# Causal mask by TensorE, one-row loads and a new order in a one-core attention and feed-forward kernel

## The chip, the cores and the metric

The kernel runs on one core of a Trainium2 chip. Each core has a matrix engine (TensorE, PE in the profile), a vector engine (VectorE, DVE), a scalar engine (ScalarE, ACT), a general one (GpSimd, POOL) and a queue engine (SyncE, SP), which work side by side and wait for each other by semaphores; 16 DMA engines move data between the main memory and the core's own memory. The metric is the device time of one execution in microseconds, the median of the runs; less is better.

## The reference

Eight batches of eight heads, 576 positions, head size 64, all float32. Causal attention with a decay that is worked out from f, then a gated feed-forward block on the 4608 tokens:

```python
log_f = np.log(np.clip(f, 0.0001, 1.0))
cum = np.cumsum(log_f, axis=-1)
scores = q @ k.T / sqrt(64) + (cum[:, :, :, None] - cum[:, :, None, :])
scores = np.where(causal, -1e9, scores)
attn = softmax(scores) @ v                       # 8 x 8 x 576 x 64
x = attn.transpose(0, 2, 1, 3).reshape(4608, 512)
xn = x / sqrt(mean(x * x) + 1e-6) * rms_g
out = (silu(xn @ w_gate) * (xn @ w_val)) @ w_out   # 512 -> 1536 -> 512
```

The decay of the key's position is multiplied into v (tile Vs, by decT) and into a column of ones beside it, so that the query's part cancels in the division; scores need no addition for it.

## The kernel before

**Tiles.** A block (b, qi) is 128 queries of all eight heads of batch b; a batch has four such blocks and a last one of 64 queries, which is joined with that of the next batch. For every block the kernel loads q, k and v, turns q and k (`turn_pe`: transposes on PE and copies by DVE and ACT, for the first eight blocks of the kernel, set by `onpe`; `turn`: a DMA transpose issued by SP, for the others), multiplies scores into a PSUM tile sc of two banks (`score_block`, L569), takes exp on ACT (L588) into PT, masks the diagonal tile, multiplies with Vs (`values`, L622, a unit for the even heads and one for the odd ones), divides (L637, L639), and norms: the sum of squares (L653 on ACT or L667 on DVE), its power on POOL (L672), xn (L679 or L683), and a transpose into xT (L692 and L699 for the first two groups, a DMA transpose at L703 otherwise).

**Groups.** Four blocks of 128 tokens make a group of 512 tokens; there are nine, the ninth from the blocks of 64. The first four blocks are block 0 of batches 0 to 3. For each group `gate` makes hidden columns from w_gate and w_val (L771; twelve gates, in the first two groups cut into tokens halves x = 0 and 1, where x = 0 needs only the first two blocks), with tanh on ACT (L784) and two products on DVE (L786, L778), and `project` multiplies by w_out (L802), copies on ACT (L814) and stores (L820, L828). The last project, of group 8, is done in two halves of 256 columns.

**The masks.** The four blocks of the first group (`FAST`) are masked on DVE by a minimum with the tile keep (L602), all later diagonal tiles on POOL (L596).

**The loads of the start.** POOL issues the q and k loads, which cast to bfloat16, and the weights; SP issues f, four v loads and rgT. For block 0 of batches 0 to 3 the q and k loads take two neighbouring rows of a head at once (`paired`, L391): 512 pieces of 512 bytes into the tiles `T_two`, which lie over ores, ga and th, turned by 16 transposes of 64 x 64 (L511). The other q and k loads take one row of a head at a time: 1024 pieces of 256 bytes (L398).

**The order.** All work is entered as units with an engine, an assumed duration, a key, dependencies and ring buffers (`Hold`). `Plan.run` plays them through once on the host: whenever an engine is free it takes the ready unit with the smallest key whose buffers are free. The order so found is the program's order on every engine. The key of each unit is moved by a number of the list SHIFTS (in hundredths of a group). The durations in the units only set this order; the chip takes its own.

Of the kernel before, what the change touches and what calls it, by code (L numbers as in the profile page):

```python
# [10 lines left out]
BF16 = mybir.dt.bfloat16  # L11
# [201 lines left out]
def fox_ffn_kernel(ctx, tc, q, k, v, f, moe_w_gate, moe_w_val, moe_w_out, moe_rms_g, out):  # L213
# [70 lines left out]

    issues = {}

    def load(eng, issue, moves, key, emit, deps=(), take=(), give=(), late=1.45):


        lane = Hold("sw" if eng == "POOL" else "hw", 1)  # L290
# [603 lines left out]
```

## Time and profile before

| | us |
|---|---|
| median of three runs | 375.93 (375.31 to 381.64) |
| the profiled execution | 376.78 |
| its span, first to last instruction | 375.1 |
| PE busy | 351.7 |
| exp on ACT (L588), 100 tiles | 99.4 |
| gate products on DVE (L786, L778) | 146.5 |
| first gate matmul (L771) | starts at 24.07 |
| last copy (L814) | starts at 371.09 |

The page's first part has the busy time of each engine; its second part cuts the span in 40 slices of about 9.4 us, each digit the busy share in tenths. A view of windows gives the same in us for chosen stretches, followed by the granted clock of PE, the DMA share and GB/s. The timeline lists instructions with their start, their duration and, in brackets, the idle time of the engine ahead of them and what ended it. The chain of waits follows the work that ended last back to the start. A tile's view gives the minimum, the median and the maximum of its instructions in ns, and the time from a DMA's issue to its landing. In the DMA view a queue q0 is that of POOL's loads and q1 that of SP's.

### The profile page before, as it was taken

The numbers are of one execution on the slowest core, as the hardware profiler recorded it, in microseconds if no ns is written. First come the engines' busy times: TensorE is split into PE (matmuls) and PEld (weight loads), VectorE is DVE, ScalarE is ACT, GpSimd is POOL, SyncE is SP. The second block draws the span as 40 slices with busy tenths as digits, with TensorE's granted clock in tenths as the row PEclk, the third lists the DMA queues.
The fourth block names the chain that finished last, engine by engine and source line by source line (L and its number), as shares of the span: only waits on it lengthen the run. The fifth ranks groups of instructions, "written<-read, shape, count | busy, mean of one in ns | idle before, by whom it ended". The sixth has DMA issues, their size and how long they took to land.

```text
span 375.1 us, 8971 instructions
## 1 busy us (share of the span) xinstructions
PE 351.7 (94%) x3569; PEld 203.7 (54%) x3617; DVE 237.1 (63%) x460; ACT 206.7 (55%) x310; POOL 190.3 (51%) x259
## 2 busy tenths in 40 slices
PE   2669999999999998999999999999999999999995
PEld 2548876677755555545455455445455544444453
DVE  6758776599766857666545667655467782473520
ACT  5544666686677657735675667336777331333122
POOL 8776999999899738843534396424112000000000
PEclk9999999999999999999999999999999999999998
DMA  9999999999999959993958999960602000201024
GB/s 127 178 204 212 207 190 166 196 152 128 161 173 183 156 84 178 179 187 63 192 97 93 165 124 139 182 100 31 136 8 56 2 16 29 82 3 56 18 49 102
DMA packets 152922, 45.05 MB, mean 120 GB/s; under 512 B 141424, under 2 KB 147312, under 8 KB 152880
## 3 DMA queue, kind: packets, MB, share of 16 engines
q0 software_dynamic: 77856, 17.83, 53.9%
q1 hardware_dynamic: 74944, 26.58, 37.0%
q8 instruction: 28, 0.46, 0.5%
q14 instruction: 14, 0.11, 0.1%
q10 hardware_dynamic: 80, 0.07, 0.1%
HBM read 38.16 MB, written 9.44 MB: 127 GB/s over the span
## 4 chain that ended last, share of the span: by engine, by line
PE 85%; DVE 6%; DMA 5%; issue 2%; ACT 1%; POOL 1%; ACTq 0%; DVEq 0%; SPq 0%
PE ff L771 47%; PE ff L802 24%; PE sc L569 7%; PE ff L622 6%; DMA rgT<-in_moe_rms_g_dram 3%; DMA QT<-qk 2%; DVE junk L667 1%; DVE x L639 1%; DVE ga L786 1%; DVE hT L778 1%; DVE Vs L327 1%; DVE xn L683 1%; PE ff L692 0%; POOL rs L672 0%; PE ff L515 0%
## 5 line engine op out<-in xcount | busy, mean ns | idle before, releaser
L588 ACT ACTIVATE PT<-sc 128x1024 bf16<-128x1024 f32 x100 | 99.4, 1022 | 41.2 <-PE sc L569 35.5
L786 DVE SCALAR_TENSOR_TENSOR ga<-th,ff 128x512 f32<-128x512 f32 x108 | 73.6, 685 | 55.2 <-ACT th L784 51.1
L802 PE MATMUL ff<-wo,hT 128*128 128x512 bf16 (+1 forms) x421 | 102.2, 373 | 1.5 <-issue 0.5
L784 ACT ACTIVATE th<-ff 128x512 f32<-128x512 f32 x108 | 64.2, 598 | 64.5 <-PE ff L771 55.5
L771 PE MATMUL ff<-xT,wg 128*128 128x512 bf16 (+1 forms) x465 | 94.0, 340 | 2.5 <-DVE rden L637 0.9
L771 PE MATMUL ff<-xT,wv 128*128 128x512 bf16 (+1 forms) x472 | 94.1, 337 | 0.8 <-DVE hT L778 0.2
L778 DVE SCALAR_TENSOR_TENSOR hT<-ga,ff 128x512 bf16<-128x512 f32 x108 | 72.9, 685 | 26.9 <-PE ff L771 20.5
L771 PEld LDWEIGHTS <-wg 128*128 128x128 bf16 x528 | 50.2, 99 | 41.7 <-issue 2.2
L771 PEld LDWEIGHTS <-wv 128*128 128x128 bf16 x528 | 50.4, 98 | 40.3 <-issue 0.3
L802 PEld LDWEIGHTS <-hT 128*128 128x128 bf16 x444 | 40.5, 98 | 41.2
L596 POOL TENSOR_SCALAR_AFFINE_SELECT PT<-PT 128x1024 bf16<-128x1024 bf16 x32 | 36.2, 1134 | 41.9 <-ACT PT L588 38.7
L540 POOL TENSOR_TENSOR Vs<-v,decT 128x512 bf16<-128x512 f32 (+1 forms) x39 | 41.7, 1069 | 24.7 <-DMA v<-in_v_dram 24.1
L814 ACT COPY ores<-ff 128x512 f32<-128x512 f32 (+1 forms) x37 | 21.1, 572 | 39.5 <-PE ff L802 39.4
L622 PEld LDWEIGHTS <-PT 128*128 128x128 bf16 (+1 forms) x960 | 32.8, 103 | 17.4 <-issue 7.2
L622 PE MATMUL ff<-Vs,PT 128*128 128x65 bf16 (+1 forms) x960 | 36.9, 196 | 4.3 <-POOL Vs L541 3.0
L672 POOL TENSOR_TENSOR rs<-ms,mhalf 128x1 f32<-128x1 f32 (+1 forms) x28 | 17.9, 639 | 38.4 <-ACT junk L653 34.5
L569 PE MATMUL sc<-QT,KT 64*128 64x128 bf16 (+1 forms) x960 | 32.4, 211 | 3.7 <-DVE rgT L321 1.8
L569 PEld LDWEIGHTS <-KT 64*128 64x128 bf16 x960 | 24.0, 95 | 18.1 <-issue 14.3
L639 DVE TENSOR_TENSOR x<-ff,rden 128x256 f32<-128x256 f32 x72 | 30.6, 424 | 2.5
L398 POOL DMA_DIRECT2D qk<-in_q_dram x36 | 31.3, 873 | 0.6 <-issue 0.5
L398 POOL DMA_DIRECT2D qk<-in_k_dram x36 | 31.3, 872 | 0.3 <-DMA wo<-in_moe_w_out_dram 0.3
L683 DVE SCALAR_TENSOR_TENSOR xn<-x,rs,rgB 128x512 bf16<-128x512 f32 x28 | 24.4, 898 | 10.6 <-POOL rs L672 10.6
(67 smaller groups left out, 165.0 us busy)
## 6 DMA issues: line engine op xcount, KB each, us to landing
out_dram<-ores SPq DMA_DIRECT2D x32, 256.0 KB, 2.4
v<-in_v_dram SPq DMA_DIRECT2D x20, 256.0 KB, 5.4
qk<-in_k_dram POOLq DMA_DIRECT2D x28, 128.0 KB, 5.6
qk<-in_q_dram POOLq DMA_DIRECT2D x28, 128.0 KB, 6.2
v<-in_v_dram POOLq DMA_DIRECT2D x12, 256.0 KB, 6.9
wo<-in_moe_w_out_dram POOLq DMA_DIRECT2D x2, 768.0 KB, 11.4
wg<-in_moe_w_gate_dram POOLq DMA_DIRECT2D x2, 512.0 KB, 11.9
wv<-in_moe_w_val_dram POOLq DMA_DIRECT2D x2, 512.0 KB, 13.7
```

What stands on the lines that cost most here:

```text
L398: nc.gpsimd.dma_start(out=T_qk[h.slot][0:n, :].rearrange("p (h d) -> p h d", d=D), in_=src[b, :, p0:p0 + n, :].rearrange("h p d -> p h d"))
L540: eng.tensor_tensor(T_Vs[hv.slot][0:n, j, :, 0:D], T_v32[h.slot][0:n, :, :], bcast(dj, D), ALU.mult)
L569: nc.tensor.matmul(t[:, par, c:c + n], lhsT=kt[r, p, kj * 128:(kj + 1) * 128], rhs=qt[r, p, qi * 128:qi * 128 + n], start=True, stop=True)
L588: nc.scalar.activation(T_PT[hp.slot].rearrange("p (a c) -> p a c", a=2), T_sc[h.slot], ACT.Exp, scale=scale)
L596: nc.gpsimd.affine_select(out=d, in_=d, pattern=[[0, 1024 // n], [1, n]], compare_op=ALU.is_ge, fill=0.0, base=0, channel_multiplier=-1)
L622: nc.tensor.matmul(po[i * n:(i + 1) * n, p, :], lhsT=T_PT[h.slot][:, c:c + n], rhs=T_Vs[hold_Vs[x].slot][:, kj, 2 * p + par, :], start=(kj ...
L639: nc.vector.tensor_tensor(d, po[:, :, 0:D], bcast(rden[par], D), ALU.mult)
L771: nc.tensor.matmul(T_ff[h.slot][:, c:c + n], lhsT=w[:, dc, fc * 128:(fc + 1) * 128], rhs=xT[:, dc, t0:t0 + n], start=(dc == 0), stop=(dc = ...
L778: nc.vector.scalar_tensor_tensor(hT, in0=three[0], scalar=0.5, in1=three[1], op0=ALU.mult, op1=ALU.mult)
L784: th = act(0.6, key - 0.1, lambda: nc.scalar.activation(T_th[ht.slot], T_ff[hg.slot], ACT.Tanh, scale=0.5), [ug], take=[ht])
L786: a = dve(0.72, key - 0.1, lambda: nc.vector.scalar_tensor_tensor(T_ga[ha.slot], in0=T_th[ht.slot], scalar=1.0, in1=T_ff[hg.slot], op0=ALU ...
L802: nc.tensor.matmul(T_ff[hf.slot][:, 0:nc0], lhsT=T_hT[hold_hT[g].slot][:, fc, j * 128:(j + 1) * 128], rhs=wo[:, fc, cols], start=(fc == 0) ...
```

## The change

- `paired`, `T_two` and the 64 x 64 transposes go: the first q and k loads take one row at a time into the ring qk, and are turned by four transposes of 128 x 128 each.
- `onpe` takes the first six blocks instead of eight: (2,1) and (3,1) are now turned by DMA.
- The first four blocks are no longer masked on DVE. keep holds 0 and -1e30, and a unit on PE adds it to the score tile ahead of the scores (two matmuls of 512 columns with the identity as weights, start set), which then accumulate.
- Vs of block 0 of batches 1 and 2 is made on DVE, and all squares of the first group on ACT. The constants on POOL (mhalf and the last column of x) become a unit of their own.
- The values of the 64-query blocks become one unit for both halves, which takes two ff banks at once.
- The last project is cut in 384 + 128 columns, the last 12 matmuls in one unit, copied by DVE; the two batches' rows of a store go in one DMA on SP. The last part of each project of group 8 waits for the end of the one before it.
- The plan's assumed durations and latencies are altered in many places, and SHIFTS is a new list of 1771 numbers.

```diff
-    return n < 8 and qi < LAST
+    return n < 6 and qi < LAST
...
-        nc.gpsimd.memset(keep, 3.0e38)
-        nc.gpsimd.affine_select(out=keep, in_=keep, pattern=[[1, 128]], compare_op=ALU.is_ge, fill=0.0, base=0,
+        nc.gpsimd.memset(keep, 0.0)
+        nc.gpsimd.affine_select(out=keep, in_=keep, pattern=[[1, 128]], compare_op=ALU.is_ge, fill=-1.0e30, base=0,
...
-    iden_f = pool(0.95, -29.5, emit_ident)
-    keeps = pool(1.4, -28.5, emit_keep)
+    iden_f = pool(0.58, -29.5, emit_ident)
+    consts = pool(0.38, -28.45, emit_const)
+    keeps = pool(0.65, -28.5, emit_keep)
...
-            h = hold_qk[b, nm, j] = Hold("two" if paired(b, j) else "qk", 1)
-            if paired(b, j):
-                def emit(src=src, h=h):
-                    nc.gpsimd.dma_start(out=T_two[h.slot],
-                                        in_=src[b, :, 0:128, :].rearrange("h (p r) d -> p h r d", r=2))
...
+            h = hold_qk[b, nm, j] = Hold("qk", 1)
...
-                if paired(b, j):
-                    for p in range(4):
-                        for r in range(2):
-                            for par in range(2):
-                                nc.tensor.transpose(tp[par * 64:par * 64 + 64, p * 128 + r * 64:p * 128 + r * 64 + 64],
-                                                    T_two[hq.slot][:, 2 * p + par, r, :], ident[0:64, 0:64])
-                    return
...
-        add, dur, eng = (dve, 0.8, nc.vector) if early else (pool, 1.5, nc.gpsimd)
+        add, dur, eng = (dve, 0.8, nc.vector) if early or (j == 0 and b in (1, 2, -1)) else (pool, 1.6 if j == 0 and b < WAVE else 1.25, nc.gpsimd)
...
-                                             rhs=qt[r, p, qi * 128:qi * 128 + n], start=True, stop=True)
+                                             rhs=qt[r, p, qi * 128:qi * 128 + n], start=(b, qi) not in FAST,
+                                             stop=(b, qi) not in FAST or p == 3)
...
+        if tiles[0][:2] in FAST:
+            h0 = holds[0]
+
+            def bias():
+                m = bass.AP(tensor=keep.tensor, offset=keep.offset, ap=[keep.ap[0], [0, 4], [1, 128]])
+                for par in range(2):
+                    nc.tensor.matmul(T_sc[h0.slot][:, par, :], lhsT=ident, rhs=m, start=True, stop=False)
+            u = pe(0.86, key - 0.6, bias, [iden, keeps] + ([last_bias[0]] if last_bias[0] else []), take=[h0])
+            last_bias[0] = u
+            deps.append(u)
...
-                if (b, qi) in FAST:
-                    def mk(hp=hp):
-                        d = T_PT[hp.slot].rearrange("p (h q) -> p h q", q=128)
-                        m = bass.AP(tensor=keep.tensor, offset=keep.offset, ap=[keep.ap[0], [0, 8], [1, 128]])
-                        nc.vector.tensor_tensor(d, d, m, ALU.min)
-                    masked[b, qi].append(dve(0.65, key, mk, [e, keeps]))
...
-        for par in range(2):
-            hpo = Hold("ff", 1)
...
+        hpos = [Hold("ff", 1) for _ in range(2)]
+        units = []
+        for pars in ((0, 1),) if qi == LAST else ((0,), (1,)):
...
-        if b < WAVE and js[0] < LAST and len(js) == 1 and (js[0] or b in (0, 1)):
+        if b < WAVE and js[0] < LAST and len(js) == 1 and (js[0] or b in ()):
...
-            hf, cols = Hold("ff", 1), slice(x * nc0, (x + 1) * nc0)
-            for part in range(3):
...
+            hf, cols = Hold("ff", 1), slice(x * 384, 384 + x * 128) if halves == 2 else slice(0, DM)
+            wide = cols.stop - cols.start
+            parts = 3 - 2 * x
+            for part in range(parts):
...
-                    deps += hdone[g, j, part] + Lo
+                    deps += hdone[g, j, part] + Lo + ([ends[-1]] if part + 1 == parts and ends else []) + (hdone[g, j, 2] if x else [])
...
+            add, copy = (dve, nc.vector.tensor_copy) if x else (act, nc.scalar.copy)
...
-            for i in range(2):
-                eng, queue = ("ACT", nc.scalar) if x + i == 2 else ("SP", nc.sync)
...
+            def st(cols=cols):
+                to = bass.AP(tensor=out.tensor, offset=out.offset + (2 * j * S + LAST * 128) * DM + cols.start,
+                             ap=[[S * DM, 2], [DM, 64], [1, cols.stop - cols.start]])
+                nc.sync.dma_start(out=to, in_=T_ores[ho.slot][:, cols])
+            load("SP", 0.4, (128, 0.0049), key, st, [c], give=[ho], late=0.7)
```

More of the change, by code (lines that the diff above doesn't have):

```diff
@@ L183, in run @@
                 n += 2
-                pair = sum(m[2] for m in moving.values()) * (1.1 if len(moving) > 1 else 1.0)
+                pair = sum(m[2] for m in moving.values())
                 first = min(moving.values(), key=lambda m: m[1])
@@ L188, in run @@
                 break
-            pair = sum(m[2] for m in moving.values()) * (1.1 if len(moving) > 1 else 1.0)
+            pair = sum(m[2] for m in moving.values())
             now, _, what, u = heapq.heappop(events)
@@ L232, in fox_ffn_kernel @@
     sizes = dict(qk=12, QT=4, v32=4, Vs=4, PT=8, x=6, xn=4, xT=2, xTr=1, hT=2, th=2, ga=2, ores=3,
-                 sc=2, ff=4, hw=8, sw=8, project=2, two=7)
+                 sc=2, ff=4, hw=8, sw=8, project=2)
     T_qk = ring("qk", sizes["qk"], [128, H * D], BF16)
@@ L285, in fox_ffn_kernel, with load @@
     issues = {}
-    def load(eng, issue, moves, key, emit, deps=(), take=(), give=(), late=1.45):
+    def load(eng, issue, moves, key, emit, deps=(), take=(), give=(), late=1.35):
         lane = Hold("sw" if eng == "POOL" else "hw", 1)
-        u = P.add(eng, issue, key, emit, deps, list(take) + [lane], (), lat=0.9 if eng == "POOL" else 0.55)
+        u = P.add(eng, issue, key, emit, deps, list(take) + [lane], (), lat=0.7 if eng == "POOL" else 0.7)
         issues[id(emit)] = u
@@ L330, in emit_ident, with emit_const @@
         make_identity(nc, ident_f)
+    def emit_const():
         nc.gpsimd.memset(mhalf, -0.5)
@@ L380, in fox_ffn_kernel @@
     late, issues_of = {}, {}
-    def paired(b, j):
-        return j == 0 and b < WAVE
     def load_qk(b, j, key):
@@ L387, in load_qk @@
         for src, nm in ((q, "q"), (k, "k")):
-            h = hold_qk[b, nm, j] = Hold("two" if paired(b, j) else "qk", 1)
-            if paired(b, j):
-                def emit(src=src, h=h):
-                    nc.gpsimd.dma_start(out=T_two[h.slot],
-                                        in_=src[b, :, 0:128, :].rearrange("h (p r) d -> p h r d", r=2))
-                qkload[b, nm, j] = load("POOL", 0.9, (512, 0.00125), key, emit, take=[h])
-                issues_of.setdefault(nm, issues[id(emit)] if nm == "k" else qkload[b, nm, j])
-                continue
+            h = hold_qk[b, nm, j] = Hold("qk", 1)
             def emit(src=src, h=h):
@@ L411, in emit @@
             queue.dma_start(out=T_v32[h.slot][0:n, :, :], in_=v[b, :, p0:p0 + n, :].rearrange("h p d -> p h d"))
-        vload[b, j] = load(eng, dur, (64, 0.022) if eng == "POOL" else (8 * n, 0.00117), key, emit, deps, take=[h])
+        vload[b, j] = load(eng, dur, (64, 0.0176) if eng == "POOL" else (8 * n, 0.00117), key, emit, deps, take=[h])
         late.setdefault((b, j), []).append(issues[id(emit)])
@@ L421, in emit @@
                 nc.gpsimd.dma_start(out=w[:, :, c0:c1], in_=src[:, c0:c1].rearrange("(c p) f -> p c f", p=128))
-            Lw[nm, i] = [load("POOL", 0.75, (512, 0.005 * (c1 - c0) / 512), key, emit, late=2.3)]
+            Lw[nm, i] = [load("POOL", 0.75, (512, 0.00247 if i < 2 else 0.0045), key, emit, late=1.2 if i < 2 else 2.2)]
     def load_wo(key):
@@ L578, in score_block @@
         cols = sum(len(items) * n / 128 for b, qi, items, n in tiles)
-        cold = all(home(b, qi)[0] == 0 for b, qi, items, n in tiles)
-        u = pe(0.19 + (0.45 if cold else 0.24) * cols, key, emit, deps, take=holds, give=gives)
+        u = pe(0.19 + 0.25 * cols, key, emit, deps, take=holds, give=gives)
         last_block[0] = u
@@ L592, in score_block @@
             masked.setdefault((b, qi), []).append(e)
-            if items[-1][1] == qi:
+            if items[-1][1] == qi and (b, qi) not in FAST:
                 def mk(hp=hp, n=n):
@@ L628, in values @@
             gives = list({id(h): h for x in xs for kj in range(qi + 1) for h in hold_PT[x, qi, kj][:1]}.values())
-            if qi == LAST and par == 1:
-                gives += [hold_Vs[x] for x in xs]
-            cost = 0.8 if qi == LAST else 0.03 + (0.12 if qi else 0.22) * (qi + 1)
-            u = pe(cost, key, emit, deps, take=[hpo], give=gives)
+            if qi == LAST:
+                gives += gives + [hold_Vs[x] for x in xs]
+            cost = 1.42 if qi == LAST else 0.03 + (0.12 if qi else 0.22) * (qi + 1)
+            u = pe(cost, key, emit, deps, take=[hpos[par] for par in pars], give=gives)
             last_val[0] = u
+            units += [u] * len(pars)
+        for par, hpo, u in zip(range(2), hpos, units):
             def ev(par=par, hpo=hpo):
@@ L684, in emit @@
                                                    in1=rgB, op0=ALU.mult, op1=ALU.mult)
-                u = dve(0.7, key - 0.02, emit, [r, L_rgB], take=[hn], give=[hx])
+                u = dve(0.78, key - 0.02, emit, [r, L_rgB], take=[hn], give=[hx])
             if g < 2:
@@ L693, in tr @@
                                             ident)
-                t = pe(0.25 if g else 0.5, key, tr, [u, iden], take=[hf], give=[hn])
+                t = pe(0.25 if g else 0.42, key, tr, [u, iden], take=[hf], give=[hn])
                 def cp(hf=hf, g=g, c=c):
@@ L704, in tr @@
                                                 in_=T_xn[hn.slot])
-                pieces[b, j] = load("SP", 1.28, (512, 0.00145), key, tr, [u], take=[hold_xT[g]], give=[hn])
+                pieces[b, j] = load("SP", 1.28, (512, 0.0013), key, tr, [u], take=[hold_xT[g]], give=[hn])
     START = (0, 1, 3, 6, 10, 13)
@@ L789, in gate @@
         return dve(0.72, key - 0.1, last, [a, uv], take=[hold_hT[g]], give=[ha, hv])
+    ends = []
     def project(g, j, key):
```

88 lines of the change are left out of this document (40 added, 48 removed), and 144 rows, old and new, of the table SHIFTS.

## The prediction

> **What bounds the kernel now.** I read the page's busy shares and slices first, then a table of windows, then the chain of waits and the timeline of the first 30 us and of the end.
>
> ```profile
> PE 351.7 (94%) x3569; PEld 203.7 (54%) x3617; DVE 237.1 (63%) x460; ACT 206.7 (55%) x310; POOL 190.3 (51%) x259
> PE   2669999999999998999999999999999999999995
> DMA  9999999999999959993958999960602000201024
> 0.00:5.00 5.00, 0.21 (x9) 0.24 (x10) 3.35 (x16) 1.64 (x2) 3.81 (x17) 1.00 0.63 82
> 5.00:10.00 5.00, 3.18 (x77) 2.75 (x72) 3.23 (x7) 4.48 (x7) 4.93 (x10) 1.00 1.33 180
> 10.00:15.00 5.00, 2.95 (x64) 2.52 (x65) 4.31 (x12) 2.44 (x4) 3.30 (x5) 1.00 1.69 173
> 15.00:20.00 5.00, 2.88 (x44) 2.29 (x44) 3.86 (x10) 2.98 (x4) 3.21 (x5) 1.00 1.48 186
> 20.00:25.00 5.00, 2.58 (x25) 2.06 (x25) 3.54 (x11) 1.44 (x3) 4.83 (x8) 1.00 1.31 204
> ```
>
> The second column of a window is its length, the third is PE's busy time. The span is 375.1 us, so PE is idle for 375.1 - 351.7 = 23.4 us. Five windows hold 4.79 + 1.82 + 2.05 + 2.12 + 2.42 = 13.2 us of it, all before 25 us. The end holds some 4.2 us (shown below). The 345 us between have 5.9 us, 1.7%. So no edit can win more than those 23.4 us unless it takes instructions off PE, and the only places with room are the first 25 us and the last four. DMA is full (tenths of 9) from the second slice of 5 us on for half of the kernel: in the start, whatever adds to a transfer moves everything queued behind it.
>
> ```profile
> 5.32 0.29 POOL L337 TENSOR_SCALAR_AFFINE_SELECT keep<-keep 128x128 bf16<-128x128 bf16 x1
> 8.93 0.64 PE L511 MATMUL ff<-ident,ores 64*64 64x64 bf16 x16
> 9.37 0.62 PE L511 MATMUL ff<-ident,ga 64*64 64x64 bf16 x16
> 14.06 0.68 DVE L602 TENSOR_TENSOR PT<-PT,keep 128x1024 bf16<-128x1024 bf16 x1
> 20.16 1.04 POOL L540 TENSOR_TENSOR Vs<-v,decT 128x512 bf16<-128x512 f32 x1 [1.96 <-DMA v<-in_v_dram]
> 21.30 0.56 POOL L672 TENSOR_TENSOR rs<-ms,mhalf 128x1 f32<-128x1 f32 x1
> 21.41 0.60 PE L622 MATMUL ff<-Vs,PT 128*128 128x65 bf16 x8 [2.97 <-POOL Vs L541]
> 21.56 0.69 DVE L699 TENSOR_TENSOR xT<-ff,rgT 128x512 bf16<-128x512 bf16 x1 [1.32 <-DMA rgT<-in_moe_rms_g_dram]
> 24.07 3.57 PE L771 MATMUL ff<-xT,wg 128*128 128x256 bf16 x16 [0.34 <-DVE xT L699]
> 30.12 1.04 PE L771 MATMUL ff<-xT,wg 128*128 128x256 bf16 x8
> 9.16 12.37 DMA rgT<-in_moe_rms_g_dram
> ```
>
> The rows are of the timeline, the last one of the chain. The first gate matmul starts at 24.07, and what is late for it is: rgT, issued at 9.16 behind four v loads, lands at 21.53; block 1's rs on POOL stands behind a Vs that waits for v until 20.16, so its xn and its piece of xT come last. PE's longest wait of the start, 2.97 us, is for that same Vs. The granted clock reads 1.00 throughout, yet 16 gate matmuls take 3.57 us at 24.07 (223 ns each) and 8 take 1.04 us at 30.12 (some 110 ns apart): PE is at half rate until about 28 us.
>
> **The change part by part.**
>
> *Bias in place of the mask.* Four DVE masks of 0.68 us go from between exp and values. Eight matmuls of 512 columns come; no row has one at the slow rate. Twice 223 ns gives 446 ns each, 3.6 us; at the fast rate, four of 512 columns go in 0.86 us (row in the last fence), so 1.7 us. I take 3.6, since the rows before 24 us are slow. They lie in PE's waits of 13.2 - 4.79 = 8.4 us before the first gate; the next paragraphs take 2.97 + 0.7 of these away, which leaves 4.7 as cover. Without it they would cost their 3.6. They wait for keep from POOL (ready near 5.6 now) and each takes one of two score buffers early.
>
> *One-row loads.* The paired transposes are 16 small matmuls, and the rows at 8.93 and 9.37 start 0.44 us apart; four of 128 columns at the slow rate take as long by the 223 ns for 256 columns (4 x 0.11). Nothing there. The loads get 1024 packets in place of 512, for the same bytes. Price by the share of the 16 engines:
>
> ```profile
> q0 software_dynamic: 1628, 0.40, 107.8%
> q1 hardware_dynamic: 691, 0.18, 22.5%
> ...
> q1 hardware_dynamic: 5446, 1.34, 96.1%
> q0 software_dynamic: 3520, 0.44, 70.0%
> ```
>
> The first two rows are the DMA view of 4 to 8 us (paired loads on q0), the others that of 120 to 130 us (one-row loads on q0). Per load: 512/1628 x 1.078 x 4 = 1.36 us against 1024/3520 x 0.70 x 10 = 2.04 us of engine time. The shares overlap (130% and 166% in all); divided by that, 1.05 and 1.23. So a load costs 0.2 to 0.7 us more; from nothing (same bytes) to 1.05 (twice the packets) if neither holds. I take 0.35, nearer to the divided figure, which is what the queue behind sees; for seven loads ahead of the first gate weights that is 2.5 us.
>
> [...]
>
> *The new order of the start.* Read off the new shifts: POOL issues k0, q0, constants, q1, identity, k1, q2, keep, k2, q3, w_gate part 0, k3, then w_gate 1, w_val 1, w_gate 2, and only then w_val 0. SP's v loads go in order of blocks, v2 ahead of v3 (now v3 goes first). Vs of blocks 1 and 2 move from POOL to DVE, squares of blocks 0 and 1 from DVE to ACT (0.8 us each, ACT is busy 11.3 of 20 us there). Identity comes later by a load issue or two; I count 0.4 us.
>
> ```profile
> L421 POOL DMA_DIRECT2D wv<-in_moe_w_val_dram x1: 842/842/842, 8.2 to 8.2; - x1
> DMA to landing us min/median/max: 8.9/8.9/8.9
> L421 POOL DMA_DIRECT2D wg<-in_moe_w_gate_dram x1: 809/809/809, 9.0 to 9.0; - x1
> DMA to landing us min/median/max: 10.5/10.5/10.5
> 27.86 1.32 PE L771 MATMUL ff<-xT,wv 128*128 128x256 bf16 x8
> ```
>
> w_gate 0 lands at 9.0 + 10.5 = 19.5, behind w_val 0 (17.1), which PE does not use before 27.86. With w_val 0 (2.4 us between the landings) and one q/k load (1.05) behind it, and 2.5 + 0.5 more for the others, it lands at 19.5 - 3.45 + 3.0 = 19.1. Block 1: its mask starts at 14.06 behind other work of DVE although exp was over near 13.4; without it values follow at once, and evacuation, squares, rs, xn, transpose and xT take an estimated 5.5 us, so 18.9, if rgT is there (v and rgT keep their queue; nothing suggests later than 21.5). First gate: 20.2, 3.9 us earlier. But block 3 now comes behind it: two transposes, bias, scores, values, one xn transpose, some 2.7 us of PE between the slow and the fast rate, where before three xn transposes (1.2 us) were left. So -3.9 + 1.5 = -2.4 us. Ends: -4.4 (all of 8.4 but the bias and 0.4 gone), +4 (loads at the double, below). The cover is x=0 gate work while block 3 arrives; if w_gate 1 is late, PE waits there.
>
> *Blocks (2,1) and (3,1) to DMA transposes.*
>
> ```profile
> 34.48 0.39 PE L515 MATMUL ff<-ident,qk 128*128 128x128 bf16 x4
> 34.71 1.04 PE L771 MATMUL ff<-xT,wv 128*128 128x256 bf16 x8
> 9.16 3.89 SPq L453 DMA_DIRECT2D rgT<-in_moe_rms_g_dram  x1
> 45.07 0.34 SPq L472 DMA_DIRECT2D rgB<-in_moe_rms_g_dram  x1
> L494 SPq DMA_TRANSPOSE QT<-qk x9: 1188/1221/1824, 55.9 to 93.7; - x9
> DMA to landing us min/median/max: 2.5/5.2/6.3
> ```
>
> Four units of four transposes leave PE, 34.71 - 34.48 = 0.23 us each, -0.9 us where PE is never idle. Four SP transposes come (1.2 us of issue each); SP's queue issues nothing between rgT (9.16 + 3.89) and rgB at 45.07, so nothing waits behind them. What is late next is their landing, 5.2 us in place of a fraction: hidden as long as other PE work stands ahead of these scores, up to 5 us if not. Ends -1.6 (with the 0.39 us of each counted) and +5.
>
> *Last-64 values in one piece.* Same matmuls; two of four ff banks at once instead of one after the other. Zero, covered by gates already in the banks; four such pieces, 0.6 us each (rden and x) if a gate must wait for a bank, +2.4 at most; -2.4 by the same row, if joining spares waits.
>
> *The last project and the end.*
>
> ```profile
> 370.02 0.37 ACT L814 COPY ores<-ff 128x256 f32<-128x256 f32 x1 [2.41 <-PE ff L802]
> 371.09 0.59 ACT L814 COPY ores<-ff 128x512 f32<-128x512 f32 x1 [0.70 <-PE ff L802]
> 371.70 0.34 SPq L820 DMA_DIRECT2D out_dram<-ores  x1
> out_dram<-ores SPq DMA_DIRECT2D x1, 256.0 KB, 2.0
> out_dram<-ores SPq DMA_DIRECT2D x1, 64.0 KB, 1.9
> 337.15 0.86 PE ff L771 x4
> ```
>
> Now a 512-wide project of group 7 ends last: copy at 371.09, store, end at 375.1, some 4.2 us behind PE. By the new shifts the 128-wide piece is last. Its copy goes by 0.37 for 256 and 0.59 for 512 columns to 0.26: -0.33; its store is 64 KB, -0.1 to -0.5. PE streams the same columns (12 x 512). I take -0.6; ends 0 and -1.
>
> *The rest of the order.* 5.9 us of idle between 25 and 370: -2 to +4, and I take zero, as no row tells which way.
>
> **Sum.** -2.4 - 0.9 - 0.6 = -3.9 us. The profiled execution took 376.78 us around its span of 375.1, so 372.9 and a span of 371.2. The median of the runs (375.93) stands 0.85 below the profiled one: 372.0.
>
> **The rivals.**
> - *The start gets dense and warm: 368.* The bias fills PE's waits before the first gate. For: PE is 58% busy there and would be over 75%; 16 matmuls at 223 instead of 110 ns cost 1.8 us at 24.07. Against: bias and waits may not meet. It wins another 1.8 plus about 2 of idle: 372.0 - 3.8 = 368.2. [...]
> - *The one-row loads are the new bound: slower, 379.* At 1.05 us more for each of seven loads, with a late w_val 0 behind them, the weights land 7.4 us late less the 3.45 that was moved away: first gate at 24.07 + 4 = 28, and the tail and transposes give back 1.5; 375.9 + 4 - 1.5 = 378.4, or 379 with a wait for w_val 0. It decides from 1.4 times the engine time per load upward if nothing overlaps. For: DMA is full there; against: q1's packets pass between q0's.
> - *A new wait takes what is won: 376.* The scores of (2,1) or (3,1) stand in PE's queue until their transposes land, up to 5 us, or longer while the q/k loads that feed them queue in a full DMA. 372.0 + 4 = 376.
>
> **How the numbers follow.** Forecast (369 to 375) 0.50, warm start (365 to 369) 0.20, new wait (374 to 378) 0.14, loads as bound (376 to 382) 0.11, a bad order elsewhere (above 382) 0.05. Leaving out a tenth below and a tenth above gives 366.5 to 378.0; the likeliest case by itself is 369 to 375. 2% of 375.93 is 7.5 us, about what a measurement of this kernel can tell from no change: below 368.4 lie half of the warm case and a little of the forecast, 0.16; above 383.4 half of the last and a little of the loads, 0.05; the rest 0.79.
>
> **What would show it.** Right: first L771 near 20 us, PE idle before 25 us near 9 in place of 13.2, no wait for Vs of 3 us, 16 L515-type transposes fewer, the last copy on DVE with 128 columns and the span's end 3.6 us behind PE. Wrong: w_gate 0 landing after 22 us (loads), a wait of PE scores for DMA QT or KT above 2 us near 45 us (transposes), PE idle between 25 and 370 above 9 us (the order), gate matmuls at 110 ns from the first (warm).

## The result and the profile after

The kernel became slower, 394.88 us (392.8 to 395.77, four runs) against 377.88 (375.31 to 381.64, four runs, on the same chip): a ratio of 1.0466 with an interval of 1.0366 to 1.0565. (Ratios leave disturbed executions out on both sides, so they can differ a little from a quotient of the medians.) The profiled execution took 392.8 us, its span is 391.1 against 375.1. One correction to the description of the change: the new SHIFTS has 1756 numbers; the list of the kernel before has 1771.

The page of the changed kernel, its busy shares, slices and the chain's shares by engine, and as a last line the chain's shares of the kernel before:

```profile
PE 354.0 (91%) x3513; PEld 199.6 (51%) x3513; DVE 235.0 (60%) x455; ACT 206.0 (53%) x311; POOL 190.0 (49%) x255
PE   3788978999989997999999999999999999999930
DMA  9999999999999999977995999852202020001111
PE 64%; POOL 13%; DMA 12%; ACT 3%; issue 2%; DVE 2%; SPq 2%; POOLq 0%; ACTq 0%; DVEq 0%
PE 85%; DVE 6%; DMA 5%; issue 2%; ACT 1%; POOL 1%; ACTq 0%; DVEq 0%; SPq 0%
```

Three things stand out. PE's slices end in 3 and 0: the last 16 us have next to no matmul. The DMA slices are full over the first 17, then end in four 1s, where DMA has nothing but stores to move. And in the chain of the work that ended last PE holds 64% where it held 85%; POOL and DMA have taken its place. Next the view of windows; columns as before (start and end, length, PE busy, and so on to the granted clock, the DMA share, GB/s):

```profile
0.00:5.00 5.00, 0.00 (x0) 0.00 (x0) 3.22 (x15) 1.52 (x2) 3.81 (x16) 1.00 0.66 66
5.00:10.00 5.00, 3.41 (x26) 2.14 (x27) 2.62 (x7) 3.08 (x5) 4.93 (x8) 1.00 1.63 177
10.00:15.00 5.00, 4.33 (x40) 2.18 (x38) 3.86 (x12) 3.26 (x5) 4.13 (x7) 1.00 1.81 193
15.00:20.00 5.00, 2.62 (x36) 1.60 (x35) 3.02 (x8) 3.67 (x8) 4.71 (x8) 0.99 1.65 175
20.00:25.00 5.00, 5.00 (x49) 3.90 (x48) 3.03 (x11) 3.72 (x7) 2.88 (x4) 0.67 1.30 204
25.00:250.00 225.00, 213.76 (x2445) 128.70 (x2443) 149.75 (x283) 136.91 (x198) 157.99 (x203) 1.00 1.35 155
375.00:392.00 17.00, 0.17 (x4) 0.00 (x0) 0.29 (x1) 0.06 (x1) 0.00 (x0) 0.60 0.11 43
```

The same long window of the kernel before:

```profile
25.00:250.00 225.00, 219.97 (x2494) 134.82 (x2526) 154.09 (x299) 142.29 (x210) 160.80 (x208) 1.00 1.29 157
```

This splits the 16.0 us of the two spans. PE ends at 375.2 (last row 0.17 us into it) instead of 370.9, and what lies behind PE grew from 4.2 to 15.9 us: 11.7. The other 4.3 us are a sum of both signs. Before 25 us PE is idle 5 + 1.59 + 0.67 + 2.38 + 0 = 9.64 us in place of 13.2 (-3.6). From 25 to 250 it is idle 225 - 213.76 = 11.24 in place of 5.03 (+6.2). PE is busy 354.0 in place of 351.7 (+2.3: bias matmuls in, some transposes out; a part of it is only that the trace of the kernel before lacks 48 matmuls, 3569 beside 3617 weight loads). The rest of the span gives -0.6. So the start won nearly what was forecast, and the middle and the end lost some five times that.

The timeline of the end:

```profile
365.47 0.68 SPq L830 DMA_DIRECT2D out_dram<-ores  x1
370.04 0.59 ACT L815 COPY ores<-ff 128x512 f32<-128x512 f32 x1 [0.28 <-PE ff L801]
370.65 10.92 SPq L830 DMA_DIRECT2D out_dram<-ores  x4
373.93 1.13 ACT L815 COPY ores<-ff 128x512 f32<-128x512 f32 x2 [3.30 <-PE ff L801]
375.26 0.29 DVE L815 COPY ores<-ff 128x128 f32<-128x128 f32 x1 [19.25 <-PE ff L801]
```

The last copy is the 128-column one on DVE, as forecast, and over at 375.55; the stores then need 15.5 us more. The DMA view of 374 to 390 us (GB/s in 40 slices, then the queue's packets, MB and share of 16 engines):

```profile
GB/s 36 36 51 51 51 51 51 51 51 51 51 51 51 51 51 51 51 51 51 51 51 51 51 51 50 47 50 54 46 54 46 54 46 54 46 46 44 44 31 12
q1 hardware_dynamic: 511, 0.77, 12.9%
```

A flat 51 GB/s, at 12.9% of sixteen engines: two engines are 12.5%. The stores that L830 issues are [2 batches][64 rows][columns], so their outermost step has only two values. At 51 GB/s a 256 KB store takes 5.1 us, and the stores of the last group, 1.05 MB, take 20.6 us, where PE ends 9.7 us after the first of them is issued (365.47 to 375.17). That the step of 2 gives each store two engines is an estimate from the 12.9%, since the trace does not name the engines; what the form of a store does to its rate is shown by the runs below.

PE's waits between 25 and 150 us (total, times, longest):

```profile
PE sc L560 <- DMA KT<-qk: 3.3, 2, 1.7
PE ff L767 <- DVE xn L679: 1.9, 1, 1.9
PE ff L617 <- POOL PT L597: 1.6, 1, 1.6
```

And the longest there in the kernel before:

```profile
PE ff L771 <- DVE rden L637: 0.9, 1, 0.9
```

The two KT waits, 1.72 us at 56.16 and 1.57 at 67.08 in the timeline, are the scores of (2,1) and (3,1), which stand behind a DMA transpose. The others are the ends of longer chains through DVE and POOL. POOL itself waits for v; over the whole span, after:

```profile
POOL Vs L531 <- DMA v<-in_v_dram: 32.4, 12, 6.6
```

### The profile page after: what moved, and what is told of

Same layout as the page of the kernel before. It is cut to its first block, busy times and chain, and to the rows that moved or that the text cites. A ratio compares the mean times of both kernels' runs of the same rounds, so it can differ in the third digit from the quotient of the medians.

```text
span 391.1 us, 8824 instructions
## 1 busy us (share of the span) xinstructions
PE 354.0 (91%) x3513; PEld 199.6 (51%) x3513; DVE 235.0 (60%) x455; ACT 206.0 (53%) x311; POOL 190.0 (49%) x255
## 4 chain that ended last, share of the span: by engine, by line
PE 64%; POOL 13%; DMA 12%; ACT 3%; issue 2%; DVE 2%; SPq 2%; POOLq 0%; ACTq 0%; DVEq 0%
PE ff L767 37%; PE ff L801 18%; DMA qk<-in_k_dram 6%; POOL qk L400 4%; PE sc L560 4%; PE ff L617 4%; DMA v<-in_v_dram 3%; DMA KT<-qk 3%; POOL Vs L531 2%; POOL PT L597 2%; POOL rs L668 1%; ACT PT L589 1%; SPq L496 1%; DVE xn L679 1%; POOL v L413 1%
## 5 line engine op out<-in xcount | busy, mean ns | idle before, releaser
L589 ACT ACTIVATE PT<-sc 128x1024 bf16<-128x1024 f32 x100 | 98.4, 1022 | 36.0 <-PE sc L560 31.9
L801 PE MATMUL ff<-wo,hT 128*128 128x512 bf16 (+2 forms) x444 | 104.6, 373 | 0.0
L767 PE MATMUL ff<-xT,wv 128*128 128x512 bf16 (+1 forms) x480 | 95.6, 337 | 0.8 <-DMA wv<-in_moe_w_val_dram 0.7
L531 POOL TENSOR_TENSOR Vs<-v,decT 128x512 bf16<-128x512 f32 (+1 forms) x37 | 39.2, 1060 | 35.4 <-DMA v<-in_v_dram 32.4
L400 POOL DMA_DIRECT2D qk<-in_k_dram x40 | 35.4, 886 | 1.2 <-POOLq L880 0.8
L400 POOL DMA_DIRECT2D qk<-in_q_dram x40 | 34.5, 865 | 2.1 <-PE ff L767 1.7
L679 DVE SCALAR_TENSOR_TENSOR xn<-x,rs,rgB 128x512 bf16<-128x512 f32 x28 | 26.9, 973 | 11.9 <-POOL rs L668 11.7
L668 POOL TENSOR_TENSOR rs<-ms,mhalf 128x1 f32<-128x1 f32 (+1 forms) x28 | 17.1, 611 | 27.9 <-ACT junk L649 21.4
```

The lines of the kernel that those rows point to most:

```text
L400: nc.gpsimd.dma_start(out=T_qk[h.slot][0:n, :].rearrange("p (h d) -> p h d", d=D), in_=src[b, :, p0:p0 + n, :].rearrange("h p d -> p h d"))
L531: eng.tensor_tensor(T_Vs[hv.slot][0:n, j, :, 0:D], T_v32[h.slot][0:n, :, :], bcast(dj, D), ALU.mult)
L589: nc.scalar.activation(T_PT[hp.slot].rearrange("p (a c) -> p a c", a=2), T_sc[h.slot], ACT.Exp, scale=scale)
L679: nc.vector.scalar_tensor_tensor(T_xn[hn.slot], in0=T_x[hx.slot][:, 0:DM], scalar=rs[:, i:i + 1], in1=rgB, op0=ALU.mult, op1=ALU.mult)
L767: nc.tensor.matmul(T_ff[h.slot][:, c:c + n], lhsT=w[:, dc, fc * 128:(fc + 1) * 128], rhs=xT[:, dc, t0:t0 + n], start=(dc == 0), stop=(dc = ...
L801: nc.tensor.matmul(T_ff[hf.slot][:, 0:wide], lhsT=T_hT[hold_hT[g].slot][:, fc, j * 128:(j + 1) * 128], rhs=wo[:, fc, cols], start=(fc == 0 ...
```

## The experiments

*Merged stores undone, all else as in the changed kernel:*

```diff
-                to = bass.AP(tensor=out.tensor, offset=..., ap=[[S * DM, 2], [DM, 64], [1, cols.stop - cols.start]])
-                nc.sync.dma_start(out=to, in_=T_ores[ho.slot][:, cols])
+                for i in range(2):
+                    t0 = (2 * j + i) * S + LAST * 128
+                    nc.sync.dma_start(out=out[t0:t0 + 64, cols], in_=T_ores[ho.slot][i * 64:(i + 1) * 64, cols])
```

> The changed kernel, but each store of the last group goes as two DMAs of 64 rows again (one per batch), both on SP; order and all else as changed. In the changed kernel PE ends at 375.17 and the span at 391.1, with the DMA share at 0.11 to 0.13 (two of 16 engines) and some 50 GB/s from about 366 us to the end. Theory A (a DMA whose target begins with a dimension of 2 is carried by two engines, so 1.05 MB at 50 GB/s is the tail): the span's end comes back to some 4 us behind PE, span 379 to 380, time 12 us below the changed kernel, near 382, within 2% of before. Rival B (the tail comes from the stores being late or few on one SP queue, whatever their shape): twice the DMAs on the same queue, no better than 391. What is left above before, some 4 us, would be the order between 25 and 150 us.

Measured: 386.24 against 376.53, ratio 1.0194 [1.0098, 1.0290]. The DMA view of the same stretch, 374 to 390 us:

```profile
GB/s 0 0 0 0 353 302 31 205 220 184 16 0 0 0 0 0 82 220 179 205 204 127 131 82 50 32 0 0 0 0 0 0 0 20 0 0 0 0 0 0
```

The timeline says which stores these are:

```profile
374.78 0.35 SPq L823 DMA_DIRECT2D out_dram<-ores  x1
375.64 7.56 SPq L830 DMA_DIRECT2D out_dram<-ores  x8
```

The first, at 353 and 302 GB/s, is a store of group 7: 256 KB in one DMA on the same queue, with 128 rows as its outermost step. The stores of 64 rows behind it go at some 200 GB/s (220 at most), with pauses between. So neither the size of a store, nor that it is one DMA, nor its queue makes the merged ones slow; what sets them apart from the store of group 7 is the outermost step of 2. Some 10 us of the loss is gone from the end (5.4 us behind PE in place of 15.9), and a loss of 1 to 3% is left.

> e1 once more beside e13, on one chip: 382 to 388 as before, 1% to 2.5% above the kernel before; it gives the difference that the half v transfers have to explain, from more runs.

The same kernel once more, on another chip: 386.91 against 376.71, 1.0278 [1.0227, 1.0330]. Against the 1.0466 of the changed kernel the merged stores are worth 1.8 to 2.7% by the two (each interval reaches a percent or less to both sides).

*Merged stores on two queues.* `nc.sync` becomes `(nc.scalar if j % 2 else nc.sync)` in the changed kernel.

> The changed kernel with its one-DMA stores of the last group sent in turn by SP (j = 0, 2) and ACT (j = 1, 3). Theory A (two engines carry each such DMA, the same two whichever queue sends it): DMA share stays near 0.12 and the span within 2 us of 391. Rival B (one queue works its DMAs off one after the other): two queues side by side take about half, GB/s near 100 and the span near 382. In between would be two other engines for the second queue.

Measured: 395.47 in one run, no gain (its span, 393.8, is 2.7 us longer than that of the changed kernel, a little outside the 2 us of the expectation). The DMA view of 378 to 392 us, ACT's queue and SP's:

```profile
q10 hardware_dynamic: 330, 0.44, 8.4%
q1 hardware_dynamic: 130, 0.26, 4.8%
```

Together 13.2%, as one queue had alone (12.9%), at a mean of 50 GB/s where it was 48: two queues moved no more than one. That they share the same two engines is an estimate from these shares. By this run SP's queue is not the limit.

*The merged store in the kernel before.*

```diff
+                    if i == 0:
+                        to = bass.AP(tensor=out.tensor, offset=..., ap=[[S * DM, 2], [DM, 64], [1, cols.stop - cols.start]])
+                        nc.sync.dma_start(out=to, in_=T_ores[ho.slot][:, cols])
-                    queue.dma_start(out=out[t0:t0 + 64, cols], in_=T_ores[ho.slot][i * 64:(i + 1) * 64, cols])
```

> The kernel before with one thing of the change: the two batches' rows of a store of the last group go in one DMA on SP. Theory A: its last-group stores go at 50 GB/s; these are 1.05 MB, the first three projects end by about 363 us there, so the tail ends near 363 + 21 = 384 against 375: 7 to 12 us slower. Rival B (the store is harmless by itself, the new order brings the tail): within 1 us of before.

Measured: 390.73 against 376.53, 1.0364 [1.0290, 1.0438]: +14.2 us from this edit alone, more than forecast. The timeline of its end says why:

```profile
363.50 13.44 SPq L830 DMA_DIRECT2D out_dram<-ores  x5
376.79 0.59 ACT L814 COPY ores<-ff 128x512 f32<-128x512 f32 x1 [4.27 <-DMA out_dram<-ores]
```

Here the slow stores also hold the ores buffers, so that the last copy waits 4.27 us for one. The changed kernel has no such wait.

*One-row loads in the kernel before, its order frozen* (the pairing and its 64 x 64 transposes removed; the eight loads get buffers of their own).

> The kernel before with the first eight q and k loads as one-row loads (into qk tiles that are free then) and their transposes as four of 128 x 128; the order of all instructions stays. Theory C (the one-row loads make DMA late in the start): the eight loads cost 0.2 to 0.7 us each in a full DMA, so w_gate 0 lands 1.5 to 5 us later than 19.5, the first gate moves with rgT and w_gate by 1 to 4 us, time 1 to 4 us up. Rival D (packets of v pass between the q/k packets and the weights are not waited for; the loss of the change lies in its order): within 1 us of before.

Measured: 380.55 against 377.81, 1.0086 [1.0050, 1.0121], by the ratio +3.2 us or 0.4 us a load. The DMA view of 4 to 8 us, POOL's queue and SP's:

```profile
q0 software_dynamic: 2560, 0.32, 126.2%
q1 hardware_dynamic: 762, 0.19, 24.1%
```

1024/2560 x 1.262 x 4 = 2.02 us of engine time a load, 1.34 divided by the share of 150%; paired it was 1.36 and 1.05. The first gate moves from 24.07 to 25.82.

*Bias in the kernel before, in place of the DVE mask, order frozen* (keep, the two bias matmuls and the start and stop flags as in the change's diff).

> The kernel before with the mask of the first four blocks done by the eight 512-column matmuls straight ahead of their scores, the DVE masks left out; the order of all else stays. By the prediction the bias lies in PE's waits and the masks' 0.7 us each go from block 0 and 1's path, but rgT, landing near 21.5, still holds the first gate: within 1 us of before, first gate near 24. If the denser PE opens its clock sooner (the warm rival), gate matmuls at 110 ns apart from the first on and 1 to 2 us less.

Measured: 377.71 against 377.81, 0.9981 [0.9940, 1.0022]. The first gate in its timeline:

```profile
23.43 2.95 PE L774 MATMUL ff<-xT,wg 128*128 128x256 bf16 x16 [0.34 <-DVE xT L702]
```

It starts 0.6 us earlier and takes 2.95 us in place of 3.57, and nothing of it is left at the end: within the 0.4% of the interval the bias costs nothing, and its earlier gate brings nothing.

*Transposes of (2,1) and (3,1) by DMA in the kernel before* (`n < 8` to `n < 6` in `onpe`).

> The kernel before with blocks (2,1) and (3,1) turned by DMA (limit 6 instead of 8), the order worked out again with the old SHIFTS. Theory E (these transposes land late in a full DMA, and their scores stand in PE's queue): PE waits for DMA KT or QT of 2 to 5 us before 70 us, as the 3.9 us in the changed kernel, time 1 to 4 us up in spite of 0.9 us less PE work. Rival D (they are covered by other work when the order places them well): within 1 us of before, no such wait over 1 us.

Measured: a median of 385.43, but six runs between 377.26 and 390.57, which gives no ratio. Five of the six lie above all 28 executions of the kernel before on that chip (375.24 to 382.23). The profiled execution is the sixth, 377.26 with 375.5 us of span, and none of the waits of PE listed for it ends with a DMA's KT or QT; the five others have no trace. So this edit seems to make the time unsteady; its size and the reason stay open.

*All parts of the change in the order of the kernel before.* The changed kernel with two stores, each unit's key set to its planned place in the kernel before, and the old plan figures of the DMAs:

```diff
-        assert len(SHIFTS) in (0, len(self.units))
-        for u, x in zip(self.units, SHIFTS):
-            u.key += 0.01 * x
+        assert len(TIMES) == len(self.units)
+        for u, x in zip(self.units, TIMES):
+            u.key = 0.1 * x
...
-        vload[b, j] = load(eng, dur, (64, 0.0176) if eng == "POOL" else (8 * n, 0.00117), key, emit, deps, take=[h])
+        vload[b, j] = load(eng, dur, (64, 0.022) if eng == "POOL" else (8 * n, 0.00117), key, emit, deps, take=[h])
```

> All parts of the change (bias, one-row loads, DMA transposes of (2,1) and (3,1), last-64 values in one unit, 384 + 128, squares and Vs moved), with two DMAs per last store as in e1, but in the order of before: each unit takes as its key the time that the plan of before gave it, and the plan's assumed DMA figures are those of before. e1 stands 7 us above before. Theory D (the new order is what costs the rest): 1 to 3 us of before, and PE idle between 25 and 150 us near 4 to 6. Rival (the parts cost it, in whatever order): 5 us or more above before, near e1.

Measured: 378.58 against 377.81, 1.0021 [0.9981, 1.0062]. With the merged stores out and the old order in, the loss is gone; so is every gain. Against the two runs with the new order (1.0194 and 1.0278) the order alone costs 1.7 to 2.6%. The windows of 25 to 250 us, first of this kernel, then of the second run of the one with two stores in the new order:

```profile
25.00:250.00 225.00, 218.01 (x2478) 132.55 (x2505) 150.51 (x297) 140.92 (x207) 158.44 (x206) 1.00 1.39 159
```

```profile
25.00:250.00 225.00, 215.97 (x2447) 129.63 (x2444) 146.77 (x284) 136.91 (x199) 158.05 (x203) 0.98 1.32 154
```

PE is idle 6.99 us here and 9.03 there; in the first run with two stores it was 16.15. What tells the orders apart better is what PE waits for. These are its listed waits of 25 to 250 us that end with the landing of a DMA, first in that second run, then in this kernel:

```profile
PE ff L767 <- DMA xT<-xn: 3.2, 1, 3.2
PE sc L560 <- DMA KT<-qk: 2.2, 2, 1.2
PE sc L560 <- DMA QT<-qk: 0.7, 1, 0.7
PE ff L510 <- DMA qk<-in_q_dram: 0.7, 1, 0.7
```

```profile
PE sc L575 <- DMA QT<-qk: 0.5, 1, 0.5
```

Together they are 6.8 us in the new order (8.5 in its first run, 4.6 in the changed kernel) and 0.5 in the old (0.5 in the kernel before too). In the new order with two stores PE's granted clock falls besides. Two windows of the second run:

```profile
50.00:60.00 10.00, 8.13 (x55) 4.46 (x53) 3.88 (x6) 4.43 (x6) 9.32 (x13) 0.83 2.20 168
110.00:120.00 10.00, 9.45 (x123) 4.96 (x124) 4.40 (x10) 4.32 (x6) 6.57 (x10) 0.83 1.64 202
```

A mean granted clock of 0.83 over 10 us is 0.17 x 10 = 1.7 us of clock that was not granted, 3.4 for the two; the first run with two stores comes to 3.4 too (0.96, 0.87 and 0.83 in three windows). The kernel before, the old order with all parts and the changed kernel read 1.00 in all such windows between 30 and 370 us. That pauses bring this about is an estimate from PE's longest waits between 25 and 250 us: 3.5 and 3.2 us in the two runs with the lower clock, 1.9 in the changed kernel.

*Half of the v loads left out* (all v loads but the first four leave out heads 4 to 7, so what is computed from these heads isn't the reference's). First in the new order with two stores, then in the old order with all parts:

```diff
-            queue.dma_start(out=T_v32[h.slot][0:n, :, :], in_=v[b, :, p0:p0 + n, :].rearrange("h p d -> p h d"))
+            queue.dma_start(out=T_v32[h.slot][0:n, 0:4, :], in_=v[b, 0:4, p0:p0 + n, :].rearrange("h p d -> p h d"))
```

> e1 (new order, two DMAs per store) with half of the v transfers left out: all v loads but the first four bring four of the eight heads, so the values of the other heads are of old data. Theory F (the new order leaves no slack for v, q and k that land late in a full DMA: POOL's queue stands 32 to 40 us at Vs for v, against 24 before, and the masks, rs and loads behind it come late): most of the 7 us between e1 and e8 goes, 378 to 380, POOL's wait for v under 15 us, PE idle from 25 to 250 us from 16 towards 6. Rival G (the new order loses by its own sequence, whatever DMA does): within 2 us of e1, 384 or more.

Measured: 375.87 against 377.26, 0.9966 [0.9936, 0.9995]: 11.0 us below the 386.91 with all of v, which ran on another chip.

> e8 (old order, all parts of the change) with the same half of the v transfers left out as in e9. e9 came from about 386 (e1) to 375.9. Theory F (late v, q and k hurt the new order because it leaves them little slack, the old one has it): e13 is 376 to 378, at most 2 us below e8's 378.6. If half of v gives the old order as much as the new (8 us or more, below 371), e9 says nothing about the order, only that DMA bounds both.

Measured: 374.27 against 376.71, 0.9932 [0.9901, 0.9963]: 4.3 us below the 378.58, between the two theories (at most 2 us, or 8 and more). POOL's waits for v, in the new order with half of v, and in the old:

```profile
POOL Vs L531 <- DMA v<-in_v_dram: 20.1, 8, 4.7
```

```profile
POOL Vs L546 <- DMA v<-in_v_dram: 19.6, 6, 8.6
```

Less traffic helps both orders. By the ratios, each against the kernel before on its own chip, it gives the new order 2.3 to 3.1% and the old one 0.9%, and the gap between the two shrinks from 1.7 to 2.6% to 0.34%. So most of what is wrong with the new order depends on the load of the DMA engines. PE's waits that end with a landing show a part of it: they fall from 6.8 to 4.5 us in the new order and stay at 0.5 in the old. POOL's total wait for v does not: 20.1 and 19.6 us here (under 15 was expected), and with all of v 26.8 in the second run of the new order beside 25.1 in the old:

```profile
POOL Vs L531 <- DMA v<-in_v_dram: 26.8, 11, 6.1
POOL Vs L546 <- DMA v<-in_v_dram: 25.1, 8, 8.8
```

How the gain of 11 us splits stays open: the two profiled executions differ by only 6.5 us of span (375.4 and 381.9), and PE's idle time of 25 to 250 us by 1.7 (7.35 and 9.03).

The next run is, despite its label, the kernel of the old order with all transfers, on the chip of the first of these two:

> e8 (old order, new parts) once more as a look beside e9 on the same chip, all transfers whole: 376 to 381, as before; it only anchors e9.

Measured: 376.95 in one run, beside 377.26 of the kernel before.

*The start of the new order, the rest of the old, (2,1) and (3,1) on PE again.* Without and with paired loads:

> The parts of the change with two stores, (2,1) and (3,1) turned on PE again, the start (loads of the weights, the first four blocks and the gates of group 0) in the order of the changed kernel, all else in the order of before moved 2.5 us ahead, with the old DMA figures. The changed kernel's first gate is at 20.95 against 24.07, PE idle before 25 us 9.6 against 13.2, less 1.8 us of bias. If that gain keeps: 374 to 376, 0.5% faster than before. If the one-row loads (3 us in e5) eat it: 377 to 380.

Measured: 381.55 against 377.26, 1.0058 [1.0010, 1.0106].

> e11 with the paired two-row loads in place of one-row loads. If the one-row loads cost here what e5 shows (0.9%): 2 to 3 us less than e11 and 1% below before, 373 to 375; if the new start hides them, the same as e11.

Measured: 384.39, 1.0120 [1.0043, 1.0196]. Neither beats the kernel before. By its ratio the first stands at 379.4 us, where the one-row loads were to put it (377 to 380); but to pair them again, which should then have won 2 to 3 us, won nothing. The first has its first gate at 21.10 (old order with all parts: 23.04), and this lead is lost again behind it: the window of 25 to 250 us has PE idle for 225 - 216.31 = 8.69 us, against 6.99.

```profile
25.00:250.00 225.00, 216.31 (x2483) 131.78 (x2513) 151.46 (x300) 140.70 (x207) 158.31 (x205) 1.00 1.32 156
```

*Paired loads in the new order, two stores.*

> The kernel of e1 with the paired two-row loads and the 64 x 64 transposes of block 0 of batches 0 to 3 put back, in the order of the changed kernel (the assumed durations of the plan stay). Theory C (one-row loads cost DMA time in the full start, 0.2 to 0.7 us each, which is what makes q, k and v late between 25 and 110 us): 2 to 4 us faster than e1, PE idle between 25 and 150 us falls from 9.8 towards 5. Rival D (the idle there comes from the order itself and from the plan's assumed latencies): within 1 us of e1, PE idle between 25 and 150 unchanged.

Measured: 383.77 against 376.53, 1.0133 [1.0040, 1.0226]. Its interval overlaps that of one-row loads (1.0194), and in the pair above pairing went the other way: no verdict on the loads in the new order. Its profiled execution has PE idle for 5.85 us of 25 to 150 us, where the two with one-row loads have 11.11 and 7.09.

## Why the prediction was wrong

The forecast was 372.0 with a range to 378.0; the time is 394.88, outside of all cases but the last, "a bad order elsewhere", which had 0.05. That case names only a part of it: some half of the loss is the form of a store. The working failed in two of its steps, which had only small ends.

**The last project and the end** stood at -0.6 with ends 0 and -1. It cost 7 to 10 us (1.8 to 2.7%). The step counted the copy and the bytes of the last store, 64 KB, and priced the store by rows in which a 256 KB store lands in 2.0 us. Those stores have 128 rows as their outermost step and go at up to 353 GB/s. The new pattern has an outermost step of 2, and goes at 51 GB/s. The diff showed that pattern, and the step asked only how many bytes were last, not how they are spread. What was said of the copy was right (last on DVE, 128 columns). Its gain did not come with the 64-row stores either: the profiled runs of these have 5.3 to 5.4 us behind PE, not 3.6; in the new order eight of them are issued behind the last store of 128 rows, from 375.64 to 383.20 in the first run.

**The rest of the order** stood at 0 with ends -2 and +4, "as no row tells which way". It cost 6.5 to 9.7 us (1.7 to 2.6%). The test named for it came out: PE idle between 25 and 370 above 9 us (11.2 of it before 250). The step before it, the transposes of (2,1) and (3,1), supplies a part: two waits of 3.3 us together, inside its upper end of +5. Its own test, a wait above 2 us, was not met in the changed kernel (1.72 at most) and was met in the first run with two stores (3.41); the same transposes in the old order give PE no such wait. So it is the order that lets PE stand at landings, for 4.6 to 8.5 us between 25 and 250 in place of 0.5, and in two of its runs the granted clock falls on top (to 0.83 over 10 us). That taking half of v away closes most of the gap between the orders supports this; which entries of the plan made the new order tight was not tried. POOL waits longer for v in the changed kernel, 32.4 us where it was 24.1 (row below), but the 26.8 and 25.1 of the two orders with two stores show that this sum alone does not decide. The new plan's DMA figures are lower than the old (0.0176 in place of 0.022 for a v load, and a factor of 1.1 for transfers that meet is gone), which would make a planner count on earlier landings, but this is only argued.

POOL's waits for v in the kernel before:

```profile
POOL Vs L540 <- DMA v<-in_v_dram: 24.1, 13, 4.4
```

**The new order of the start** came out close in size, and worthless at the end. First gate at 20.95 (20.2 forecast), PE idle before 25 us 9.64 (near 9), w_gate 0 landed at 17.5 (19.1). A part of this was luck: rgT, without which no gate can start, was put at "nothing suggests later than 21.5", which would not allow a gate at 20.2. It landed 3.5 us earlier, and why is not shown:

```profile
18.04 0.69 DVE L695 TENSOR_TENSOR xT<-ff,rgT 128x512 bf16<-128x512 bf16 x1 [1.08 <-DMA rgT<-in_moe_rms_g_dram]
```

The old order with all parts has its first gate at 23.04, and the one with the new start at 21.10 ends no earlier for that: the lead is eaten between 25 and 250, where PE waits for later loads. The view of waits of the kernel before, with PE 94% busy, did not show that the loads behind PE had no room; the DMA slices at 9 for half of the span did.

**One-row loads.** 0.35 us each, 2.5 for seven; measured 3.2 for eight, 0.4 each. Right. The doubling, the upper end of 1.05 us more a load, did not come: 2.02 against 1.36 us of engine time, 1.5 times before overlap and 1.3 after it.

**Bias.** Hidden, at the slow rate, 3.6 us; measured 3.7 us for eight in the changed kernel, and no change of the time when alone. That the two sums meet is luck in part: not all of the eight ran at the slow rate (two of them took 0.59 us, last section).

```profile
L571 PE MATMUL sc<-keep,ident 128*128 128x512 bf16 x8 | 3.7, 565 | 0.0
```

**Rivals.** "A new wait takes what is won" had the mechanism of the middle, with 4 us too small a price, and as a single wait where there are many. "The one-row loads are the new bound" did not hold. "Dense and warm" came half: the clock opened before the first gate (two bias matmuls in 0.59 us at 14.56, after 1.04 at 11.82), but closed again (0.50 granted from 20 to 23 us, last section). That a denser PE opens it sooner is an estimate: PE was busy for 4.33 of the 5 us from 10 us on, where it had been 2.95 and still ran at half rate at 24.07 (223 ns a gate matmul, 110 at 30.12). The rival that decided the end, a transfer that becomes slower by its form, was not among them.

## What to carry to other kernels

Merging two stores saves an issue (0.68 us on SP for the first of the merged ones, 1.18 for the two in its place), but look at the outermost step of the new pattern: with two steps there the stores went at 51 GB/s here, 12.9% of sixteen engines, in place of some 200. When DMA is full for half of a span, a gain in the first 25 us can be lost again behind it, as it was here, so test a new order against the new operations in the old order before believing either. A forecast of "zero, no row tells" needs ends as wide as the largest wait that the fullest resource can make.

## What was not expected of the hardware

A second queue added nothing to the merged stores (13.2% of sixteen engines and 50 GB/s from two queues, in one run; 12.9% and 48 GB/s from one).

The clock closed here without a long pause: 0.50 was granted from 20 to 23 us, and no gap of PE in the six us before was longer than 0.69 us. Rows of PE's timeline in the changed kernel:

```profile
11.82 1.04 PE L571 MATMUL sc<-keep,ident 128*128 128x512 bf16 x2
14.56 0.59 PE L571 MATMUL sc<-keep,ident 128*128 128x512 bf16 x2
20.95 1.89 PE L767 MATMUL ff<-xT,wg 128*128 128x256 bf16 x8
24.08 1.04 PE L767 MATMUL ff<-xT,wv 128*128 128x256 bf16 x8
```

Two bias matmuls of the same form take 1.04 us, and the next two 0.59: the clock opened between 12 and 14.5 us. Eight gate matmuls take 1.89 us at 20.95 and 1.04 at 24.08: it had closed and opened again. The windows between (the granted clock is the third number from the end):

```profile
14.00:18.00 4.00, 1.87 (x22) 1.12 (x22) 2.71 (x9) 2.84 (x7) 2.93 (x5) 1.00 1.80 164
18.00:20.00 2.00, 1.33 (x19) 0.82 (x20) 1.31 (x2) 1.83 (x3) 2.00 (x4) 0.97 1.43 197
20.00:23.00 3.00, 3.00 (x29) 2.19 (x28) 1.19 (x5) 2.04 (x5) 2.54 (x4) 0.50 1.29 206
```

From 14 to 18 us PE is busy for 47%, with no single gap longer than 0.69 us, and from 20 us on the granted clock is 0.50. The column alone does not show every closed clock: from 10 to 15 us it reads 1.00, where the first pair of bias matmuls took 1.04 us. In the first run with two stores the clock stayed open (1.00 granted over the first 25 us), and the first eight gate matmuls took 1.05 us. In the changed kernel a half-busy stretch of some 4 us came before the clock closed, and no idle one; what closed it is not shown.
